# Batches 0 and 1 of a fused sliding-attention and MLP kernel: 1 KB runs for their tokens, fewer clears, weights loaded in eighths between tokens, their mask added by TensorE, and one norm for both dilated heads

## The chip, the cores and the metric

The kernel runs on one core of one Trainium2 chip. The metric is the device time of one execution in microseconds. Engines are named as in the profile: PE (TensorE, matrix multiplications; PEld its weight loads), DVE (VectorE), ACT (ScalarE), POOL (GpSimd), SP (SyncE, which issues nearly all transfers). Each engine works through its own instructions in the order in which they were written; semaphores between engines make an instruction wait for others.

## What is computed

Sliding-window attention, then a two-layer MLP over all 4,608 tokens. Heads 0 to 3 are plain (a query sees the 32 keys up to its own), heads 4 to 7 dilated (32 keys in steps of 4):

```python
# q, k, v: (8 batches, 8 heads, 576 tokens, 64), float32
rel = pos[:, None] - pos[None, :]
mask_plain = (rel >= 0) & (rel < 32)
mask_dil = (rel >= 0) & (rel < 32 * 4) & (rel % 4 == 0)
scores = np.where(masks, 0.125 * q @ k.T, -1e9)
attn = softmax(scores) @ v
x = attn.transpose(0, 2, 1, 3).reshape(4608, 512)
h = x @ w_in                        # 512 -> 2048
out = np.maximum(0.01 * h, h) @ w_out   # 2048 -> 512, float32
```

All matmuls take fp16 operands; inputs are float32 and are cast on the chip.

## The kernel before

**Attention.** Tokens of a head are put in groups of four, 144 groups a batch. A visit is one batch and one pair of heads (hp 0 and 1 plain, 2 and 3 dilated). Its queries and keys are loaded by group (`stg`), cast to fp16 (`nat`), turned by TensorE and copied from PSUM into `qbd` (queries of both heads, block-diagonal, zeros beside them) and `kt` (keys). A unit is a third of a visit: scores on TensorE into the single bank `sps` (L641, L625), exponential on ACT into `ee` (L646), a multiplication of `ee` by a 0/1 mask on DVE or, for batches 0 and 1, DVE or POOL (L660), values on TensorE into `ops` (L680, L670). The value tiles `vp` and `vd` hold ones beside the values, so the sums of the softmax come out too. ACT makes their reciprocal with a logarithm (L688) and an exponential (L691) in `rc`, and DVE multiplies the result into `xt` (L697), once for each head.

**MLP.** A chunk is 384 tokens, three chunks to a pair of batches, 12 in all. An up step (L717) is four matmuls of 384 columns for one of 16 blocks of 128 hidden values, into `hps`; ACT applies the leaky ReLU into `gt` (L724). A down quarter (L757) is four matmuls of 512 columns into `fps`; four of them make 128 tokens, which DVE copies to `osb` (L766) for the store. The two banks `fps` also take warm-up matmuls (L776) and fillers (L831), which keep TensorE running where the planner saw a gap.

**The first two batches** (`EARLY = 2`) are treated apart. Part 0 of a batch is its first 96 groups and part 1 the last 48 (`load_rest`, tile `rest`). Chunk 0 holds part 0 of batch 0, chunk 1 that of batch 1, chunk 2 both parts 1. Dilated heads are loaded in runs of 1 KB (a group of four tokens), plain heads in runs of 256 B (one token). Batches 2 to 7 are loaded in runs of 128 B for queries and keys and turned by DVE (L521, L532).

**Clears** (`clear`, L239). `qbd` and `kt` (all columns), `vst` (the value staging tile, in partitions that no transfer fills), `rest`, and the ones in `vp` and `vd`.

**Weights** (`load_w`). Each matrix comes in four parts of 1 MB, staged in tiles that are free at that time (`wst`, `gt` 1 and 2, `xt` 1) and cast by POOL or DVE.

**What sets the order.** All work is recorded as tasks with a priority, engines that may do it, and an assumed duration; `_Plan.run` simulates the engines and writes the instructions in the order that comes out. For transfers, `took` gives an assumed time by the length of a run. `FIRST` sets the priority of early loads, letter by letter: `b` and `c` are the token groups of batches 0 and 1, `0` and `1` their rests, `i` and `o` the weights of the two layers. `RANKS` gives the priority of the early attention parts, `WHEN` that of later batches. So instructions stand in a fixed order on each engine, and one that waits holds all behind it.

Of the kernel before, what the change touches and what calls it, by code (L numbers as in the profile page):

```python
# [17 lines left out]
FIRST = "b0ico1"  # L18
RANKS = ((-100.0, 1.0), (-50.0, 1.0), (-40.0, 1.0), (-30.0, 1.0))


def _constants():
# [12 lines left out]
    rel1 = 96 + c1 - (32 + p)  # L35
    d1 = (rel1 >= 0) & (rel1 < WIN)
    parts = [ident, first, band, band, d0, d1]
# [95 lines left out]
def kernel(  # L133
# [23 lines left out]
    EARLY = 2  # L157
# [20 lines left out]
    NCON = 128 + 288 + 96 + 48  # L178
# [5 lines left out]
    NST, NNAT, NVS, NV, NT, NE, NR, NO, NG = 5, 3, 4, 3, 6, 4, 3, 3, 3  # L184
    PAD = 32
    stg = [sbuf(f"stg{i}", [128, 1280], FP32) for i in range(NST)]
    nat = [sbuf(f"nat{i}", [128, 1152]) for i in range(NNAT)]
    vst = [sbuf(f"vst{i}", [128, 2048], FP32) for i in range(NVS // 2)]
# [3 lines left out]
    kt = [sbuf(f"kt{i}", [128, PAD + S + 64]) for i in range(NT)]  # L192
# [5 lines left out]
    rest = sbuf("rest", [128, 1792])  # L198
# [16 lines left out]
    def took(n, size):  # L215
        for a, ta, b, tb in ((4, 9.0, 128, 14.0), (128, 14.0, 256, 20.5), (256, 20.5, 1024, 60.0),
                             (1024, 60.0, 2048, 90.0)):
            if size <= b:
                return n * (ta + (tb - ta) * (size - a) / (b - a)) / 16e3
        return n * size / 23.5 / 16e3  # L220

    def load(queue, dst, src, n, size, deps, prio):
        eng = ENG[queue]
        return plan.dma(queue, 0.7 if size == 128 else 0.48, took(n, size), deps,
                        lambda e: eng.dma_start(dst, src), prio,  # L225
                        LATE if prio > -1482 else 0.0)
# [27 lines left out]
    for i in range(NT):  # L254
        p = -1900 + i
        t_zero[i] = ([clear("DVE", qbd[i][64:128, 0:S], 0.33, 0.0, p),
                      clear("DVE", qbd[i][0:64, S:2 * S], 0.33, 0.0, p)],
                     [clear("DVE", kt[i], 0.4, 0.0, p)])
    t_ones = {}
    for i in range(NV):  # L260
        p = -1800 if i == 0 else -700
        t_ones["p", i] = clear("POOL", at(vp[i], 0, 128, D, [128, 12], [1, D]), 0.75, 1.0, p)
        t_ones["d", i] = clear("POOL", at(vd[i], 0, 128, D, [128, 16], [1, D]), 0.95, 1.0, p)
# [11 lines left out]
    kept = {}  # L275

    def v_stage(n, users):

        old = []
        for i in range(n):  # L280
            k, w = ring("VST", NVS, users)
            old = old + w + t_vz[k]
            first = k if i == 0 else first
        return vst[first // 2][:, first % 2 * 1024:first % 2 * 1024 + n * 1024], old

    def heads_of(b, vi):
        if b < EARLY:
            return 2 * vi, 2 * vi + 1
        return 4 * (vi // 2) + vi % 2, 4 * (vi // 2) + vi % 2 + 2

    def load_group(b, g, prio):
# [7 lines left out]
        for o, src in ((0, q), (1, k)):  # L299
# [3 lines left out]
            if early and dil:  # L303
# [15 lines left out]
        vs, v_old = v_stage(1 if early else 2, v_users := [])  # L319
        if dil:  # L320
            lv = [load("SP", at(vs, 0, 96, 0, [256 if early else 512, 4], [1, 256]),
                       dram(v, base, [4 * D, 96], [HS, 4], [1, 256]), 384, 1024, v_old, prio)]
            if not early:
                lv.append(load("SP", at(vs, PAD, 112, 256, [512, 4], [1, 256]),
                               dram(v, base + 256 * D, [4 * D, 80], [HS, 4], [1, 256]),
                               320, 1024, v_old, prio))
        elif early:
            lv = [load("SP", at(vs, PAD, 128, hd * 256, [D, 4], [1, D]),
                       dram(v, base + hd * HS, [D, 96], [96 * D, 4], [1, D]),
                       384, 256, v_old, prio) for hd in range(4)]  # L330
# [5 lines left out]
        for j in range(2):  # L336
            nn, n_old = ring("NAT", NNAT, n_users := [])
            na, c_qk = nat[nn], []
            for o in range(2):
                st, s_users = stage[o]  # L340
                if early and dil:
                    dst = at(na, 0, 96, o * 512, [D, 2], [128, 4], [1, D])
                    src = at(st, 0, 96, j * 512, [256, 2], [D, 4], [1, D])
                    n = 512
                elif early:
                    dst = at(na, 0, 128, o * 384, [128, 3], [1, 128])
                    src = at(st, 0, 128, j * 128, [256, 3], [1, 128])
                    n = 384
                else:
# [8 lines left out]
            full, n = (8, 4 if early else 8) if dil else (6, 4 if early else 6)  # L358
            hd, step = (2 * j, 1) if early else (j, 2)
            c_v = [cast(at(vt, 0, 128, 0, [full * 128, 2], [128, n], [1, D]),  # L360
                        at(vs, 0, 128, hd * n * D, [step * n * D, 2], [D, n], [1, D]), 2 * n * D,
                        (lv if dil or not early else lv[2 * j:2 * j + 2]) + d_old, prio)]
            if not dil:
                c_v.append(cast(at(vt, 0, PAD, 128, [full * 128, 2], [128, n - 1], [1, D]),
                                at(vs, 96, 128, hd * n * D, [step * n * D, 2], [D, n - 1], [1, D]),
# [514 lines left out]
```

## Time and profile before

| | us |
|---|---|
| three runs | 341.18, 345.12, 343.71 |
| their median | 343.71 |
| the profiled execution, time | 340.5 |
| the profiled execution, span | 338.7 |
| mean granted TensorE clock in it | 0.979 |

The span runs from the first to the last instruction of the profile; 1.8 us of the time lie around it. In the profile's rows a group reads: line, engine, operation, output<-inputs with sizes, count, then busy time, mean ns of one, and the idle time of the engine just before, with what ended it. A row of a timeline reads: start in us, duration in us, engine, line, operation, count, and in brackets the idle time before it. The chain of work that ended last gives 63% of the span to PE, 9% to ACT, 7% to DMA, 6% to DVE and 5% to SP's queue.

### The profile page before, as it was taken

What the parts mean: (1) busy time and instruction counts of PE and PEld (TensorE: products, weight loads), DVE (VectorE), ACT (ScalarE), POOL (GpSimd) and SP (SyncE); (2) the same over time, 40 slices, a digit from 0 to 9 for tenths busy, and PEclk for the clock granted to TensorE, in tenths of its full rate; (3) what the DMA queues carried; (4) which work ended last, traced back from release to release, by engine and by line L of the source; (5) the groups of instructions that cost most, each with busy time, mean ns of one, the idle gap of its engine ahead of it and who ended that gap; (6) DMA issues with size and microseconds to landing.
All of it is one profiled execution on the core that took longest, in us unless ns stands there. A gap on an engine that the chain in (4) does not pass through costs nothing.

```text
span 338.7 us, 6427 instructions
## 1 busy us (share of the span) xinstructions
PE 310.6 (92%) x2239; PEld 184.2 (54%) x2239; DVE 189.8 (56%) x449; ACT 233.6 (69%) x522; POOL 140.8 (42%) x194
## 2 busy tenths in 40 slices
PE   7576886899999999999989888999999999999994
PEld 3454553465777666655555545555555555555541
DVE  7788679676688687876656648463444330100011
ACT  2388997485889999986768777777788863334310
POOL 9957538217478566764665655621000000000000
PEclk9859999799999999999999999999999999999999
DMA  8999999999999999999999999931111111111113
GB/s 188 208 316 327 188 313 268 174 217 148 171 188 138 166 158 187 151 154 176 175 153 200 176 144 197 151 79 33 43 50 34 34 31 31 33 40 55 31 31 93
DMA packets 159631, 47.87 MB, mean 141 GB/s; under 512 B 142832, under 2 KB 150896, under 8 KB 159600
## 3 DMA queue, kind: packets, MB, share of 16 engines
q1 hardware_dynamic: 159056, 46.94, 76.7%
q10 hardware_dynamic: 544, 0.54, 0.7%
q8 instruction: 17, 0.28, 0.4%
q14 instruction: 14, 0.11, 0.2%
HBM read 38.02 MB, written 9.44 MB: 140 GB/s over the span
## 4 chain that ended last, share of the span: by engine, by line
PE 63%; ACT 9%; DMA 7%; DVE 6%; SPq 5%; issue 3%; POOL 3%; DVEq 0%; POOLq 0%; ACTq 0%
PE fps L757 29%; PE hps L717 27%; SPq L225 5%; DMA stg<-in_q_dram 4%; PE sps L641 3%; PE ops L680 2%; ACT rc L688 2%; ACT rc L691 2%; DMA vst<-in_v_dram 2%; ACT gt L724 2%; ACT ee L646 2%; DVE xt L697 1%; DMA stg<-in_k_dram 1%; POOL vp L235 1%; ACT qbd L490 1%
## 5 line engine op out<-in xcount | busy, mean ns | idle before, releaser
L717 PE MATMUL hps<-xt,w_in 128*128 128x384 f16 (+1 forms) x832 | 151.3, 314 | 1.3 <-ACT gt L724 1.2
L757 PE MATMUL fps<-w_out,gt 128*128 128x512 f16 x576 | 147.8, 382 | 1.6 <-DVE w_out L235 1.4
L724 ACT ACTIVATE gt<-hps 128x384 f16<-128x384 f32 (+1 forms) x208 | 94.7, 464 | 46.0 <-PE hps L717 44.1
L717 PEld LDWEIGHTS <-w_in 128*128 128x128 f16 x832 | 76.3, 98 | 44.9 <-issue 2.0
L757 PEld LDWEIGHTS <-gt 128*128 128x128 f16 x576 | 54.9, 98 | 49.7 <-issue 3.7
L697 DVE TENSOR_TENSOR xt<-ops,rc 64x192 f16<-64x192 f32 x192 | 61.0, 343 | 31.6 <-ACT rc L691 30.2
L688 ACT ACTIVATE rc<-ops 64x384 f32<-64x384 f32 x96 | 46.5, 487 | 18.0 <-PE ops L680 12.1
L766 DVE COPY osb<-fps 128x512 f32<-128x512 f32 x36 | 24.7, 687 | 60.8 <-PE fps L757 60.5
L646 ACT ACTIVATE ee<-sps 128x384 f16<-128x384 f32 x96 | 46.7, 487 | 9.7 <-PE sps L641 8.7
L660 DVE TENSOR_TENSOR ee<-ee,con 128x384 f16<-128x384 f16 x88 | 39.2, 449 | 24.5 <-ACT ee L646 23.3
L691 ACT ACTIVATE rc<-rc 64x384 f32<-64x384 f32 x96 | 49.5, 517 | 1.5
L526 POOL COPY qbd<-turned 64x576 f16<-64x576 f16 x48 | 34.9, 728 | 26.8 <-DVE turned L521 24.2
L235 POOL CAST nat<-stg 128x576 f16<-128x576 f32 (+2 forms) x54 | 34.5, 665 | 24.9 <-DMA stg<-in_q_dram 19.9
L641 PE MATMUL sps<-qbd,kt 128*128 128x192 f16 x160 | 27.6, 255 | 5.6 <-ACT ee L646 4.3
L235 POOL CAST vp<-vst 128x768 f16<-128x768 f32 (+3 forms) x32 | 23.4, 749 | 15.1 <-DMA vst<-in_v_dram 7.5
L641 PEld LDWEIGHTS <-kt 128*128 128x128 f16 x160 | 15.8, 105 | 16.6 <-issue 6.0
L521 DVE STREAM_TRANSPOSE turned<-nat 128x576 f16<-128x576 f16 x24 | 18.2, 768 | 11.6 <-POOL nat L235 11.4
L532 DVE STREAM_TRANSPOSE kt<-nat 128x576 f16<-128x576 f16 x24 | 18.1, 763 | 7.0 <-POOL nat L235 6.9
L235 POOL CAST vd<-vst 128x1024 f16<-128x1024 f32 (+1 forms) x20 | 18.4, 945 | 6.8 <-DMA vst<-in_v_dram 3.6
L680 PEld LDWEIGHTS <-vp 128*128 128x128 f16 x192 | 13.0, 98 | 13.9 <-issue 3.9
L680 PE MATMUL ops<-ee,vp 128*128 128x96 f16 x192 | 16.0, 206 | 4.8 <-DVE ee L660 2.9
L660 POOL TENSOR_TENSOR ee<-ee,con 128x384 f16<-128x384 f16 x8 | 9.0, 1128 | 12.1 <-ACT ee L646 10.4
(60 smaller groups left out, 151.0 us busy)
## 6 DMA issues: line engine op xcount, KB each, us to landing
stg<-in_q_dram SPq DMA_DIRECT2D x48, 144.0 KB, 5.2
stg<-in_k_dram SPq DMA_DIRECT2D x48, 144.0 KB, 4.6
vst<-in_v_dram SPq DMA_DIRECT2D x6, 576.0 KB, 6.6
vst<-in_v_dram SPq DMA_DIRECT2D x8, 384.0 KB, 5.7
out_dram<-osb SPq DMA_DIRECT2D x16, 192.0 KB, 2.4
vst<-in_v_dram SPq DMA_DIRECT2D x8, 320.0 KB, 5.5
out_dram<-osb SPq DMA_DIRECT2D x24, 96.0 KB, 2.4
gt<-in_moe_w_in_dram SPq DMA_DIRECT2D x2, 1024.0 KB, 11.9
```

What stands on the lines that cost most here:

```text
L235: ENG[e].tensor_copy(out=dst, in_=src)
L526: lambda e, p0=p0, hh=hh: nc.gpsimd.tensor_copy(out=at(qb, p0, p0 + 64, hh * S + o, *od), in_=at(xb, p0, p0 + 64, i, *id_)), prio)
L641: nc.tensor.matmul(st[:, 192 * i:192 * i + 192], ka, qa, start=True, stop=True)
L646: lambda e: nc.scalar.activation(out=et, in_=st[:, 0:384], func=AF.Exp, scale=SCALE), prio + 0.1)
L660: ENG[e].tensor_tensor(out=io, in0=io, in1=mk, op=ALU.mult)
L680: nc.tensor.matmul(ot[:, c:c + 96], va, et[:, c:c + 96], start=True, stop=True)
L688: lambda e: nc.scalar.activation(out=rt, in_=ot[64:128, 0:384], func=AF.Ln),
L691: lambda e: nc.scalar.activation(out=rt, in_=rt, func=AF.Exp, scale=-1.0),
L697: nc.vector.tensor_tensor(out=at(xt[m % 2], h % 2 * 64, h % 2 * 64 + 64, h // 2 * 1152 + x, *o_), in0=at(ot, 0, 64, c, *i_), in1=at(rt, 0, ...
L717: nc.tensor.matmul(ht[:, 0:n], w_in[:, i * DFF + j * 128:i * DFF + j * 128 + 128], at(xt[m % 2], 0, 128, i * 1152 + x0 + x, [1, n]), start ...
L724: lambda e: nc.scalar.activation(out=gt[c % NG][:, j * n_c + x:j * n_c + x + n], in_=ht[:, 0:n], func=AF.Prelu, alpha=0.01),
L757: nc.tensor.matmul(ft, g[:, j * n_c + tt * 128:j * n_c + tt * 128 + 128], w_out[:, j * DM:j * DM + DM], start=(j == 0), stop=(j == NJ - 1))
```

## The change

- Plain heads of batches 0 and 1 are loaded by groups of four tokens too, in runs of 1 KB, for both parts; values of plain heads come at once for the whole batch, in runs of 256 B. The transposes for plain visits take four blocks of 96 like those of the dilated.
- `kt` is cleared only in its first 32 columns. `rest` needs no clear, and `vst` one, which ACT makes. There are seven `qbd`/`kt` pairs instead of six.
- Weights come in 16 parts of 0.5 MB; `FIRST` puts them between the tokens. Part 1 of batch 1 gets rank 20 instead of -30.
- For batches 0 and 1 the mask is not multiplied any more. TensorE first writes 0 or -60000 for each score into `sps` (a matmul of the identity with a table), and the scores are added to it in the bank.
- Dilated units use 96 or 80 keys instead of 128 partitions, for all batches; late dilated values are cast in two instructions instead of one. Heads pair as 4·(hp // 2) + hp % 2 and that plus 2 in all batches, so one DVE instruction norms both heads of a dilated unit; plain units keep two.
- `took` assumes 16 ns instead of 14 for a run of 128 B, 22 instead of 20.5 for 256 B, 100 instead of 90 for 2 KB. The table of constants grows from 560 to 992 columns.

```diff
-FIRST = "b0ico1"
-RANKS = ((-100.0, 1.0), (-50.0, 1.0), (-40.0, 1.0), (-30.0, 1.0))
+FIRST = "bbiii0ciiiciooioooooo1"
+RANKS = ((-100.0, 1.0), (-50.0, 1.0), (-40.0, 1.0), (20.0, 1.0))
...
-                     [clear("DVE", kt[i], 0.4, 0.0, p)])
+                     [clear("DVE", kt[i][:, 0:PAD], 0.1, 0.0, p)])
...
-t_rz = clear("POOL", rest[:, 768:1792], 0.9, 0.0, -1700)
-t_vz = []
-for i in range(NVS):
-    part = vst[i // 2][:, i % 2 * 1024:i % 2 * 1024 + 1024]
-    e = "POOL" if i < 2 else "DVE"
-    t_vz.append([clear(e, part[96:128, :], 0.9, 0.0, -1850),
-                 clear(e, part[0:PAD, :], 0.9, 0.0, -1850)])
+t_vz = add("ACT", 1.4, 0.2, [t_warm],
+           lambda e: nc.scalar.copy(out=at(vst[1], 0, PAD, 0, [512, 3], [1, 512]),
+                                    in_=at(warm, 0, PAD, 0, [0, 3], [1, 512])), -1990)
...
-            elif early:
-                lo = [load(queue, at(st, 0, 128, m * 256, [D, 4], [1, D]),
-                           dram(src, base + m * 128 * D, [D, 128], [HS, 4], [1, D]),
-                           512, 256, s_old, prio) for m in range(3)]
...
+w_home = [(gt[2], 0, None), (gt[2], 1024, None), (wst[0], 0, None), (wst[0], 1024, None),
+          (gt[1], 0, None), (gt[1], 1024, None), (gt[1], 2048, None), (xt[1], 0, None),
+          (xt[1], 1024, None), (wst[0], 0, 2), (wst[0], 1024, 3), (gt[1], 0, 4),
+          (gt[1], 1024, 5), (gt[1], 2048, 6), (xt[1], 0, 7), (xt[1], 1024, 8)]
...
+            if by_pe:
+                if small:
+                    bias = at(con, 0, 128, NMASK + M_D1, [0, 8], [1, 48])
+                elif dil:
+                    bias = at(con, 0, 128, NMASK + M_D0, [0, 4], [1, 96])
+                else:
+                    bias = at(con, 0, 128, NMASK + M_PL + (0 if u == 0 else 96),
+                              [96, 2], [0, 2], [1, 96])
+                nc.tensor.matmul(st[0:kn, 0:384], ident[:, 0:kn], bias, start=True, stop=False)
...
-        t_m = add((("DVE", 0.39), ("POOL", 0.9)) if b < EARLY else "DVE", 0.39, 0.15,
-                  [t_e, t_con], mask, prio + 0.1)
+        t_m = t_e if by_pe else add("DVE", 0.39, 0.15, [t_e, t_con], mask, prio + 0.1)
...
-    gt_free = {1 - NG: w_used[1], 2 - NG: w_used[4]}
+    gt_free = {1 - NG: sum(w_used[11:14], []), 2 - NG: w_used[0] + w_used[1]}
```

DVE at the start of the program, before (numbers behind a name are those of the buffer; stg holds float32 tokens, nat their fp16 form):

```order
L239 MEMSET qbd_85 64x288 x2
L239 MEMSET kt_91 128x336
L239 MEMSET vst_73 32x1024 x4
L235 CAST nat_69<-stg_64 96x2x4x64
L235 CAST nat_69<-stg_66 128x384
```

And with the change:

```order
L241 MEMSET qbd_86 64x288 x2
L241 MEMSET kt_93 128x16
L237 CAST nat_69<-stg_64 96x2x4x64
L237 CAST nat_70<-stg_65 96x2x4x64
L468 COPY qbd_80<-tp 64x4x96
```

The four clears of vst ahead of DVE's first cast are gone, and that of kt is of 16 words instead of 336.

SP's queue from the rest of batch 0 on, before (wst, gt and xt are where weights are staged):

```order
L225 DMA stg_64<-in_q_dram 48x4x256
L225 DMA stg_64<-in_k_dram 48x4x256
L225 DMA wst_110<-in_moe_w_in_dram 128x4x512
L225 DMA gt_102<-in_moe_w_in_dram 128x4x512
L225 DMA gt_103<-in_moe_w_in_dram 128x4x512
L225 DMA xt_100<-in_moe_w_in_dram 128x4x512
L225 DMA stg_65<-in_q_dram 96x4x256
```

And with the change, from the fourth part of the up weights to the last one of them:

```order
L227 DMA wst_112<-in_moe_w_in_dram 128x2x512
L227 DMA gt_104<-in_moe_w_in_dram 128x2x512
L227 DMA vst_72<-in_v_dram 96x4x256
L227 DMA gt_104<-in_moe_w_in_dram 128x2x512
L227 DMA stg_67<-in_q_dram 96x4x256
L227 DMA stg_68<-in_k_dram 96x4x256
L227 DMA vst_73<-in_v_dram 96x12x64 x2
L227 DMA gt_104<-in_moe_w_in_dram 128x2x512
L227 DMA xt_102<-in_moe_w_out_dram 128x2x512
L227 DMA wst_112<-in_moe_w_out_dram 128x2x512
L227 DMA xt_102<-in_moe_w_in_dram 128x2x512
```

The up weights stood together ahead of batch 1's tokens; their last eighths now stand behind those tokens and behind two eighths of the down weights.

ACT where batch 1's part 0 ends, before (rc are reciprocals, gt what leaves the leaky ReLU; gt_102 belongs to chunk 1, whose predecessor's 16 activations all stand further ahead):

```order
L688 ACTIVATE rc_97<-ops_115 64x384
L691 ACTIVATE rc_97<-rc_97 64x384
L490 COPY qbd_84<-tp 64x4x48
L490 COPY kt_90<-tp 128x4x48
L724 ACTIVATE gt_102<-hps_116 128x384
L646 ACTIVATE ee_92<-sps_113 128x384
```

And with the change (gt_103 is chunk 0, gt_104 chunk 1):

```order
L651 ACTIVATE rc_99<-ops_117 64x384
L654 ACTIVATE rc_99<-rc_99 64x384
L685 ACTIVATE gt_103<-hps_118 128x384
L685 ACTIVATE gt_103<-hps_119 128x384
L685 ACTIVATE gt_103<-hps_118 128x384
L685 ACTIVATE gt_103<-hps_119 128x384
L685 ACTIVATE gt_104<-hps_118 128x384
```

Four of chunk 0's activations moved behind the last reciprocal of batch 1's part 0, and the copies for part 1 moved further back.

More of the change, by code (lines that the diff above doesn't have):

```diff
@@ L571, in turn @@
-        k_apart = not (dil and part == 1)
-        tq = add("PE", 0.06 * (4 if dil else 3 if part == 0 else 2), 0.25,
-                 c_qk + [t_con] + q_old, pe_q, prio, 0.2)
-        n_users.append(tq)
-        new = []
-        if dil:
-            w = 96 if part == 0 else 128
-            o, od = lo, [[144, 4], [1, hi - lo]]
-            i, id_ = 0, [[w, 4], [1, hi - lo]]
-        else:
-            o, od, i, id_ = arranged(False, lo, hi)
-            i = 0
-        for hh in range(2):
-            p0 = 64 * hh
-            new.append(move(at(qb, p0, p0 + 64, hh * S + o, *od), at(tpb, p0, p0 + 64, i, *id_),
-                            4 * (hi - lo), [tq] + old + zq, prio))
@@ L587, in turn @@
-        if not k_apart:
-            new.append(move(at(kb, 0, 128, o, *od), at(tpb, 0, 128, 64, *id_), 4 * (hi - lo),
-                            [tq] + old + zk, prio))
-        elif part == 1:
-            new.append(move(kb[:, PAD + 512:PAD + S], tpb[:, 192:256], 64, [tq] + old + zk, prio))
+                    nc.tensor.transpose(bank[:, s * 96:s * 96 + 96],
+                                        na[0:96, c + s * step:c + s * step + 128],
+                                        ident[0:96, 0:96])
```

367 lines of the change are left out of this document (169 added, 198 removed).

## The prediction

> **What bounds the kernel now.** I read the page first, then busy time in stretches, then the timeline of the first 70 us, the groups by shape, the DMA traffic of short windows, and last the chain of the late part.
>
> ```profile
> PE 310.6 (92%) x2239; PEld 184.2 (54%) x2239; DVE 189.8 (56%) x449; ACT 233.6 (69%) x522; POOL 140.8 (42%) x194
> PEclk9859999799999999999999999999999999999999
> 10.00:20.00 10.00, 6.17 (x48) 4.44 (x47) 7.46 (x17) 5.13 (x11) 8.30 (x13) 0.68 1.14 205
> 20.00:30.00 10.00, 7.02 (x73) 5.69 (x73) 8.95 (x25) 9.02 (x23) 6.80 (x9) 0.81 1.04 380
> 50.00:60.00 10.00, 6.11 (x45) 3.18 (x44) 9.67 (x22) 6.82 (x15) 7.84 (x9) 1.00 1.15 288
> 60.00:70.00 10.00, 9.19 (x66) 4.79 (x64) 6.86 (x18) 5.56 (x14) 3.36 (x5) 0.83 1.12 156
> sum 80.00, PE 74.38 PEld 43.21 DVE 50.78 ACT 61.38 POOL 49.05; mean PE 18.60 PEld 10.80 DVE 12.69 ACT 15.35 POOL 12.26
> 212.41 0.65 PE hps L717 x4
> 213.06 0.86 PE fps L757 x4
> ```
>
> The columns of a stretch are PE, PEld, DVE, ACT, POOL, granted clock, DMA share, GB/s; the sum row is that of 140 to 220 us. The last two are from the chain: an up step is 0.65 us, a quarter of a down tile 0.86. TensorE bounds the whole, and it gives time away in two places: about 40 us before 66 us, and 80 - 74.4 = 5.6 us between 140 and 220. Behind 220 it is full.
>
> ```profile
> 7.20 0.62 ACT L233 CAST nat<-stg 96x512 f16<-96x512 f32 x1 [5.19 <-DMA stg<-in_k_dram]
> 7.94 0.91 DVE L239 MEMSET vst<- 32x1024 f32 x1 [0.25 <-DMA stg<-in_q_dram]
> 11.46 0.91 DVE L239 MEMSET vst<- 32x1024 f32 x1 [0.24 <-issue]
> 12.30 0.35 DVE L235 CAST nat<-stg 96x512 f16<-96x512 f32 x1
> 13.09 0.96 ACT L490 COPY qbd<-tp 64x384 f16<-64x384 f16 x2 [3.25 <-PE tp L543]
> 32.50 0.81 PE L717 MATMUL hps<-xt,w_in 128*128 128x384 f16 x4
> 65.05 1.03 PE L757 MATMUL fps<-w_out,gt 128*128 128x512 f16 x4
> 65.91 0.81 PE L717 MATMUL hps<-xt,w_in 128*128 128x384 f16 x4
> 13.00:62.60 49.60, 41.89 (x95) 0.88 1.08 274
> L691 ACT ACTIVATE rc<-rc 64x384 f32<-64x384 f32 x20 | 10.3, 518 | 0.3
> L646 ACT ACTIVATE ee<-sps 128x384 f16<-128x384 f32 x20 | 9.8, 490 | 2.8 <-PE sps L641 2.6
> L688 ACT ACTIVATE rc<-ops 64x384 f32<-64x384 f32 x20 | 9.6, 487 | 2.9 <-PE ops L680 2.5
> L724 ACT ACTIVATE gt<-hps 128x384 f16<-128x384 f32 x16 | 7.5, 490 | 0.5 <-PE hps L717 0.2
> L490 ACT COPY qbd<-tp 64x384 f16<-64x384 f16 x7 | 3.3, 473 | 4.1 <-PE tp L543 3.3 <-DVE qbd L492 0.7
> L490 ACT COPY qbd<-tp 64x192 f16<-64x192 f16 x4 | 1.2, 310 | 0.1
> ```
>
> Queries could have been cast at 7.2 us (keys were), but VectorE stood in its clears until 12.30. From there ScalarE sets the pace (row of 13.00 to 62.60: 41.9 of 49.6 us): 20 units of attention, the last of which lets chunk 1 start, at 65.91. Until 32.50 no useful large matmul ran. So the milestone that I follow is chunk 1's first up step.
>
> **Start of the chain.** VectorE loses the four clears of vst (7.94 to 12.30) and most of each kt clear; two q clears are added.
>
> ```profile
> 1.25 0.30 DVE L239 MEMSET qbd<- 64x288 uint32 x1
> 1.57 0.34 DVE L239 MEMSET kt<- 128x336 uint32 x1
> 2.03 0.30 DVE L239 MEMSET qbd<- 64x288 uint32 x1
> ```
>
> A round of three took 1.16 us; seven rounds without most of kt's 0.34 take about 0.85 each, from 0.86 to 6.8 us (8.9 if a small clear cost as much as a large one). ScalarE's new clear (1,536 columns, at 0.62 us for 512 below 1.9 us) lies in its 5.19 us of waiting. Late next is the key load: the constants ahead of it on ACT's queue grow by 111 KB, 0.5 to 1 us by the rates below, so I put its landing at 8.0, its cast to 8.6 and ScalarE's first copy at 8.7, 4.4 us earlier than 13.09. POOL's clears before its first cast fall too (four of vst, one of rest).
>
> **ScalarE until chunk 1.** By the order it now does 20 units of 0.490 + 0.487 + 0.518 (29.9), 12 of the 16 activations of chunk 0 (5.9), five copies of 0.473 (2.4) and six of about 0.31 (1.9): 40.1 us. It waited 49.6 - 41.9 = 7.7 us. What goes of that is the mask step between exponential and value matmul:
>
> ```profile
> L660 DVE TENSOR_TENSOR ee<-ee,con 128x384 f16<-128x384 f16 x88 | 39.2, 449 | 24.5 <-ACT ee L646 23.3
> L660 POOL TENSOR_TENSOR ee<-ee,con 128x384 f16<-128x384 f16 x8 | 9.0, 1128 | 12.1 <-ACT ee L646 10.4
> L697 DVE TENSOR_TENSOR xt<-ops,rc 64x192 f16<-64x192 f32 x192 | 61.0, 343 | 31.6 <-ACT rc L691 30.2
> ```
>
> 16 of the 88 on VectorE (7.2 us) and all 8 on POOL (9.0 us) go. They stand in each unit's latency; with four exponentials in flight I let 3.2 of the 7.7 us go and keep 4.5 (bounds 0 and 9). So the last reciprocal of batch 1's first part ends at 8.7 + 40.1 + 4.5 = 53.3. Behind it, by ScalarE's order, stand chunk 0's last four activations, and on TensorE two up steps and a down quarter: 53.3 + 0.5 + 2 x 0.65 + 0.86 = 56.0 for chunk 1's first up step, against 65.91. But then only 3 down quarters are done instead of 6 (2.6 us), and four mask matmuls are still to come (4 x 0.16). Net gain 9.9 - 2.6 - 0.6 = **6.7 us** (bounds 2 and 11). By the same count the first up step of all comes at 8.7 + 14.0 (8 units, five copies) + 2 of waiting + 0.7 of norm, near 26, against 32.50.
>
> The second part of batch 1 moves from ahead of chunk 1's steps to among them (its rank goes from -30 to 20): its four units then run beside up and down steps. Plain pairs are turned by four and four transposes instead of three and three, on a TensorE that waits: nothing.
>
> The mask matmul has no row. An up matmul of 384 columns (0.65 / 4 = 0.16 us) is nearest, twice that where the clock is halved: 24 of them, 3.9 to 7.8 us. Twenty lie before chunk 1's start, where TensorE waits for ScalarE; the other four are in the sum. The merged norm for dilated heads is one instruction of twice 192 columns, two of 0.343 at most: VectorE's time falls by up to 0.3 us a unit, beside ScalarE, at nothing. The dilated value cast of late batches becomes two instructions on POOL, 61% busy in 140 to 220: nothing.
>
> **Transfers.** Short windows of nearly one size each:
>
> ```profile
> DMA packets 1715, 0.42 MB, mean 211 GB/s; under 512 B 1715, under 2 KB 1715, under 8 KB 1715
> DMA packets 480, 0.47 MB, mean 233 GB/s; under 512 B 27, under 2 KB 480, under 8 KB 480
> DMA packets 1359, 2.71 MB, mean 387 GB/s; under 512 B 45, under 2 KB 45, under 8 KB 1357
> ```
>
> They are 11 to 13, 33 to 35 and 22 to 29 us: runs of 256 B, 1 KB and 2 KB. Per early batch the change takes 1 KB runs from 1,856 to 3,008 and 256 B runs from 7,168 to 2,304: from 1.90 / 0.233 + 1.83 / 0.211 = 16.9 us to 13.2 + 2.8 = 16.0. That is 0.9 us a batch, since the larger run moves only a tenth faster here. The Trainium skill ("DMA: Bandwidth & Descriptors", Specifications) has line rate from 512 B on and an HBM limit of about 358 GB/s; by it the 1 KB runs would take 8.6 us a batch instead of 13.2, and the sum would be that of rival (d). The trace disagrees: 233.
>
> Weights: up weights in eighths behind tokens. Ahead of the last needed up eighth stand, by SP's order, 5.5 MB of weights and constants at 387 (14.2 us), 5.05 MB of 1 KB runs (21.7) and 1.18 MB of 256 B runs (5.6): with a start near 2.6 and 1.5 of latency it lands near 45.5, 8 us before ScalarE needs it. In the old order all up weights came before batch 1. So the loads hide behind ScalarE, and moving them gains nothing by itself. One wait is new: chunk 1's activations write gt 1, where three down-weight eighths are staged; these land four eighths of 1.35 us later, near 51, and are cast near 53. Late, they would hold ScalarE's queue, with batch 1's second part behind it; 3 us are left.
>
> **Late part.** From 150 to 208 us the chain leaves TensorE:
>
> ```profile
> 155.81 5.19 DMA stg<-in_q_dram
> 182.53 4.58 DMA stg<-in_q_dram
> 200.91 4.58 DMA stg<-in_k_dram
> PE ops L680 <- DVE ee L660: 4.5, 5, 1.4
> ```
>
> The last row is TensorE's waits in 100 to 220 us: the fixed order put late attention where its tokens had not landed. The planner now books 128 B runs at 16 instead of 14 and output rows at 100 instead of 90, so it writes attention later against the matmuls, which leaves fewer such waits. It can also only move them. I take half, **2.8 us** (bounds -2 and 5.6).
>
> **Sum.** 338.7 - 6.7 - 2.8 = 329.2 us of span, with the 1.8 around it (340.5 - 338.7) 331.0. The profiled execution was 0.7 to 4.6 us faster than the three runs, 3.2 than their median; I add 2: **333 us**.
>
> **Rivals.** (a) The transfers pace it: the late chain above runs through loads, so what the start gains is waited for later; only 1.8 us of DMA time are saved: 336.9 of span, 341. For it speaks a DMA share above 1 up to 220 us; against it that TensorE waited only 5.6 of 80 us there. (b) ScalarE waits as before (7.7 us): gain 3.5 + 2.8, about 336. The single score bank now also holds the mask matmul, which speaks for it. (c) Slower: VectorE's queue behind weight casts. By its order the casts of the late eighths stand ahead of batch 1's last norms; if the last up eighth lands after 53 instead of 45.5, norms, output banks and TensorE wait one for one. From 67 on the kernel is more than 1% slower than before; at 70 the time is about 350. That needs transfers to take half as long again as the rows give. (d) 1 KB runs at the 2 KB rate (387): loads far ahead, no late waits: about 330. No row has it, and one row (233) speaks against it; the page on DMA named above would have it so. (e) ScalarE never waits and no late waits: 326.
>
> On the clock: it was 0.68 and 0.81 in 10 to 30 us and 0.83 in 60 to 70, each after thin TensorE work. The Trainium skill ("TensorE: Matmul & The Clock Gate", Part 1) halves the rate after an idle window of about 3.4 us; the trace agrees with the halving. By the order, fillers (L831) ahead of the first up step fall from 57 to 41, so a halved window may fall at chunk 1's start: 1.7 us, inside the range.
>
> **Chances.** Forecast (329 to 337) 0.55; (a) 0.14; (b) 0.12; (c) 0.05; (d) 0.04; (e) 0.10. The range 325 to 341 leaves out (c), half of (e), and part of (a). A measurement of this kernel tells about 1% from no change: faster than 340.3 are the forecast, (b), (d), (e): 0.80; (a) is within 1%: 0.14; slower 0.06.
>
> **What would show it.** In the new profile: VectorE's first cast below 8 us and ScalarE's first copy near 8.7; first up step near 27; chunk 1's first up step near 56; no mask rows before 60 us; ScalarE busy about 90% from 9 to 53; TensorE above 76 of 80 us in 140 to 220. Wrong would be a first up step as late as 32, a w_in cast that VectorE waits for while norms stand behind it, or a 140 to 220 stretch with more idle TensorE than now.

## The result, and the profile after

The changed kernel takes 331.04 us (median of four runs, 328.35 to 332.14) where the old one takes 343.0 (341.18 to 345.12): a ratio of 0.9638, with a 95% interval of 0.9553 to 0.9722. Measured again later, against other runs of the old kernel, it was 0.9647 [0.9607, 0.9687]. The profiled execution took 328.35 us, with a span of 326.5.

The page of the changed kernel: busy time of the engines, the granted clock in 40 slices, and the shares of the chain that ended last.

```profile
PE 309.6 (95%) x2258; PEld 187.3 (57%) x2258; DVE 176.5 (54%) x386; ACT 230.2 (70%) x512; POOL 128.9 (39%) x192
PEclk9699999999999999999999999999999999999998
PE 83%; ACT 9%; DMA 3%; DVE 2%; issue 2%; ACTq 0%; DVEq 0%
```

TensorE's work is about the same (309.6 us against 310.6), in a span that is 12.2 us shorter. Its clock was low in one slice near the start; the second low window that the old profile had near 65 us is not there. The next rows are busy time in stretches of the changed kernel (PE, PEld, DVE, ACT, POOL, granted clock, DMA share, GB/s), and the sum over 140 to 220 us.

```profile
10.20:52.80 42.60, 35.20 (x332) 24.96 (x333) 30.33 (x74) 37.09 (x83) 19.99 (x29) 0.92 1.12 280
60.00:70.00 10.00, 10.00 (x91) 6.31 (x90) 5.76 (x15) 6.82 (x16) 2.44 (x4) 1.00 1.05 155
sum 80.00, PE 79.92 PEld 48.46 DVE 55.95 ACT 69.74 POOL 49.28; mean PE 19.98 PEld 12.12 DVE 13.99 ACT 17.43 POOL 12.32
```

In 140 to 220 us TensorE now idles 0.1 us instead of 5.6. Most of the rest of the 12.2 us is won before 66 us. The timeline of the changed kernel (start, duration, engine, line, operation):

```profile
6.45 0.46 DVE L237 CAST nat<-stg 96x512 f16<-96x512 f32 x1
9.56 0.62 ACT L235 CAST nat<-stg 96x512 f16<-96x512 f32 x1 [6.06 <-DMA stg<-in_k_dram]
10.28 0.47 ACT L466 COPY qbd<-tp 64x384 f16<-64x384 f16 x1
12.27 0.49 ACT L610 ACTIVATE ee<-sps 96x384 f16<-96x384 f32 x1
29.75 1.47 PE L678 MATMUL hps<-xt,w_in 128*128 128x384 f16 x8
52.26 0.52 ACT L654 ACTIVATE rc<-rc 64x384 f32<-64x384 f32 x1
54.64 1.03 PE L718 MATMUL fps<-w_out,gt 128*128 128x512 f16 x4
55.50 0.81 PE L678 MATMUL hps<-xt,w_in 128*128 128x384 f16 x4
```

The last row is chunk 1's first up step, the milestone of the prediction: 55.50 instead of 65.91. The sixth is the last reciprocal of batch 1's first part, which lets it start. So 10.4 us were won there; 3.2 of them are paid back, since three down quarters (3 x 0.86) that used to lie ahead of chunk 1, and four mask matmuls (4 x 0.16) that the old kernel did not have, lie behind its start. That leaves 7.2 us of start and 12.2 - 7.2 = 5.0 behind it. This split is a rough one: by TensorE's idle time alone, 5.2 us went before 66 us and 5.5 between 140 and 220.

### The profile page after: what moved, and what is told of

Read it like the earlier page. It is cut to its first block, busy times and chain, and to the rows that moved or that the text cites. A ratio compares the mean times of both kernels' runs of the same rounds, so it can differ in the third digit from the quotient of the medians.

```text
span 326.5 us, 6336 instructions
## 1 busy us (share of the span) xinstructions
PE 309.6 (95%) x2258; PEld 187.3 (57%) x2258; DVE 176.5 (54%) x386; ACT 230.2 (70%) x512; POOL 128.9 (39%) x192
## 4 chain that ended last, share of the span: by engine, by line
PE 83%; ACT 9%; DMA 3%; DVE 2%; issue 2%; ACTq 0%; DVEq 0%
PE fps L718 38%; PE hps L678 35%; PE sps L604 4%; PE ops L643 3%; DMA stg<-in_k_dram 3%; ACT rc L651 2%; ACT ee L610 2%; ACT rc L654 2%; ACT gt L685 2%; PE sps L588 1%; PE ops L633 1%; PE sps L585 1%; ACT qbd L466 1%; DVE xt L659 0%; DVE ee L624 0%
## 5 line engine op out<-in xcount | busy, mean ns | idle before, releaser
L718 PE MATMUL fps<-w_out,gt 128*128 128x512 f16 x576 | 145.4, 379 | 0.2 <-DVE w_out L237 0.2
L659 DVE TENSOR_TENSOR xt<-ops,rc 64x192 f16<-64x192 f32 (+1 forms) x144 | 56.0, 412 | 38.1 <-ACT rc L654 35.5
L610 ACT ACTIVATE ee<-sps 128x384 f16<-128x384 f32 (+2 forms) x96 | 46.5, 485 | 12.2 <-PE sps L604 9.8
L624 DVE TENSOR_TENSOR ee<-ee,con 128x384 f16<-128x384 f16 (+2 forms) x72 | 33.6, 468 | 31.8 <-ACT ee L610 31.2
L237 POOL CAST nat<-stg 128x576 f16<-128x576 f32 (+1 forms) x55 | 36.2, 679 | 14.8 <-DMA stg<-in_q_dram 7.2
L604 PE MATMUL sps<-qbd,kt 128*128 128x192 f16 (+1 forms) x160 | 27.5, 254 | 0.0
L604 PEld LDWEIGHTS <-kt 128*128 128x128 f16 (+1 forms) x160 | 18.6, 124 | 14.3 <-issue 4.9
L237 POOL CAST vp<-vst 128x768 f16<-128x768 f32 (+1 forms) x32 | 24.4, 786 | 5.9 <-DMA vst<-in_v_dram 5.3
L237 POOL CAST vd<-vst 96x512 f16<-96x512 f32 (+1 forms) x32 | 19.2, 633 | 9.3 <-DMA vst<-in_v_dram 9.2
L643 PE MATMUL ops<-ee,vp 128*128 128x96 f16 x192 | 15.5, 206 | 0.6 <-DVE xt L659 0.5
L585 PE MATMUL sps<-con 128*128 128x384 f16 (+2 forms) x24 | 8.5, 354 | 4.1 <-ACT ee L610 4.1
```

The lines of the kernel that those rows point to most:

```text
L237: ENG[e].tensor_copy(out=dst, in_=src)
L604: nc.tensor.matmul(st[0:kn, 192 * i:192 * i + 192], ka, qa, start=not by_pe, stop=i == 1 or not by_pe)
L610: lambda e: nc.scalar.activation(out=et[0:kn, :], in_=st[0:kn, 0:384], func=AF.Exp, scale=SCALE), prio + 0.1)
L624: ENG[e].tensor_tensor(out=io, in0=io, in1=mk, op=ALU.mult)
L643: nc.tensor.matmul(ot[:, c:c + 96], va, et[0:kn, c:c + 96], start=True, stop=True)
L659: nc.vector.tensor_tensor(out=at(xt[m % 2], h0 % 2 * 64, h0 % 2 * 64 + 64, h0 // 2 * 1152 + x, *o_), in0=at(ot, 0, 64, c, *i_), in1=at(rt, ...
```

## The experiments

Three questions were open: what filled the late part, which of the edits made the start earlier, and whether the two are separate at all. In the table, "idle" is the time in the profiled execution in which TensorE was not busy, and "chunk 1" the start of its first up step, in us. The ratio is to the old kernel.

| kernel | ratio [95%] | chunk 1 | idle 0 to 66 | idle 140 to 220 |
|---|---|---|---|---|
| old | 1 | 65.91 | 17.3 | 5.6 |
| changed | 0.9638 [0.9553, 0.9722] | 55.50 | 12.1 | 0.1 |
| changed, again | 0.9647 [0.9607, 0.9687] | 55.06 | 12.6 | 0.1 |
| old, new transfer costs | 0.9714 [0.9664, 0.9764] | 62.07 | 17.8 | 0.2 |
| changed, old transfer costs | 0.9707 [0.9648, 0.9766] | 58.39 | 12.1 | 2.2 |
| old, allowance of 6 us | 0.9902 [0.9869, 0.9935] | 66.53 | 17.2 | 4.4 |
| old, no clears on VectorE | 0.998 [0.9942, 1.0018] | 64.06 | 17.6 | 5.0 |
| old, clears apart | 1.0015 [0.9987, 1.0042] | 63.23 | 14.1 | 6.2 |
| changed, clears back on VectorE | 0.9732 [0.9686, 0.9778] | 59.94 | 12.9 | 1.7 |
| changed, weights in one line | 0.9708 [0.9661, 0.9755] | 57.90 | 14.3 | 2.3 |
| changed, 256 B runs | 0.9631 [0.9583, 0.9678] | 58.02 | 15.5 | 0.0 |
| changed, mask by VectorE | 0.9571 [0.9531, 0.9611] | 56.94 | 11.3 | 1.0 |
| same, keys first | 0.9619 [0.9576, 0.9663] | 56.82 | 13.6 | 0.1 |
| changed, copies on VectorE | 0.9612 [0.9574, 0.965] | 56.11 | 12.7 | 0.6 |

**The planner's costs.** First the three numbers in `took`, alone and taken back.

```diff
-((4, 9.0, 128, 14.0), (128, 14.0, 256, 20.5), (256, 20.5, 1024, 60.0), (1024, 60.0, 2048, 90.0))
+((4, 9.0, 128, 16.0), (128, 16.0, 256, 22.0), (256, 22.0, 1024, 60.0), (1024, 60.0, 2048, 100.0))
```

> The kernel before with the new transfer times alone. Mine: TensorE's idle time from 140 to 220 us falls from 5.6 to below 2 us, chunk 1's first up step stays at 64 to 68 us, time 1 to 1.7% below the kernel before (337 to 340). Rival: without the rest of the change the late waits stay at 4 us or more and the time is that of before.

> The changed kernel, but the planner's transfer times as before (128 B runs 14, 256 B 20.5, 2 KB 90). Mine: the start keeps its gain (chunk 1's first up step at 55 to 58 us), and the 5.5 us that TensorE won between 140 and 220 us come back as waits: 2.5 to 5.5 us of idle there, time 1 to 1.7% above the changed kernel. Rival (the late waits went because attention starts earlier, or for the one norm and the removed masks, not for the costs): idle there stays below 1 us and the time is the same.

In the old kernel these three numbers alone, which change no work but only its order and the choice of engine, bring 2.9%, where the whole change brings 3.6%. That is more than the 1 to 1.7% expected, and chunk 1 came at 62.07, ahead of the 64 to 68 expected. Taken back in the changed kernel they cost only some 0.6%, less than expected, with 2.2 us of late idle time where 2.5 to 5.5 were expected. The busy time of the old kernel with them, and then of the changed kernel without them, in 140 to 220 us:

```profile
sum 80.00, PE 79.83 PEld 47.62 DVE 60.91 ACT 69.73 POOL 45.63; mean PE 19.96 PEld 11.90 DVE 15.23 ACT 17.43 POOL 11.41
```

```profile
sum 80.00, PE 77.77 PEld 46.01 DVE 53.10 ACT 63.65 POOL 49.97; mean PE 19.44 PEld 11.50 DVE 13.27 ACT 15.91 POOL 12.49
```

The old kernel's late idle time falls from 5.6 to 0.2 us. Its start idles as before (17.8 against 17.3): chunk 1 comes 3.8 us earlier, and three down quarters (2.6 us) that stood ahead of it now stand behind. In the chain of the changed kernel without the new costs, transfers come back:

```profile
165.03 5.04 DMA stg<-in_q_dram
178.61 3.84 DMA stg<-in_q_dram
191.82 4.50 DMA stg<-in_q_dram
210.73 4.44 DMA stg<-in_k_dram
```

With the new costs no load stands in the chain between 138 and 222 us, in either kernel. So the theory on the late part holds in kind, though its sizes were off, and the rival that the costs only move waits falls. But the two halves don't add: the costs alone bring 2.9%, everything else alone 2.9%, both 3.6%.

If late attention is simply written too early, another way to book loads later should do the same. The planner's allowance for the landing of a late load went from 4 to 6 us, in the old kernel:

```diff
-AHEAD, LATE = 5.0, 4.0
+AHEAD, LATE = 5.0, 6.0
```

> The old kernel with the planner's allowance for the landing of a late load raised from 4 to 6 us, and its three transfer costs as they were. Theory (the late waits come from an order that put late attention where its tokens had not landed, so that any way of booking them later does): TensorE busy 78 to 80 of 80 us in 140 to 220 instead of 74.4, the time 1 to 1.7% below the old kernel's. Rival (it is the cost of the rows themselves, which spreads transfers against each other, and not the allowance, that matters): 74 to 76 of 80 us, the time within 0.5%.

One per cent was won, the low end of what the theory expected, but TensorE was busy 75.59 of 80 us, as the rival expected, and the chain still ran through five loads:

```profile
sum 80.00, PE 75.59 PEld 44.29 DVE 53.96 ACT 63.78 POOL 50.56; mean PE 18.90 PEld 11.07 DVE 13.49 ACT 15.95 POOL 12.64
```

```profile
171.12 4.95 DMA stg<-in_q_dram
177.24 6.05 DMA vst<-in_v_dram
189.53 3.02 DMA stg<-in_k_dram
198.49 2.12 DMA stg<-in_q_dram
210.05 4.89 DMA stg<-in_q_dram
```

A fixed allowance is therefore not the same as a cost for each run, which adds up over the loads that queue behind one another. That this adding up is the reason was not tried, nor which of the three numbers does it.

**The mask on TensorE.** The mask of the first two batches was multiplied by VectorE or GpSimd again.

```diff
-by_pe = b < EARLY
+by_pe = False
...
-t_m = t_e if by_pe else add("DVE", 0.39, 0.15, [t_e, t_con], mask, prio + 0.1)
+t_m = add((("DVE", 0.39), ("POOL", 0.9)) if b < EARLY else "DVE", 0.39, 0.15,
+          [t_e, t_con], mask, prio + 0.1)
```

> The changed kernel, but the mask of batches 0 and 1 multiplied by VectorE or GpSimd again, none added by TensorE. Mine: ScalarE waits 2 to 4 us more up to the last reciprocal of batch 1's first part, chunk 1's first up step at 57 to 60 instead of 55.5, time 0.5 to 1.2% above the changed kernel. Rival (the mask matmul on the one score bank costs what the multiplication did): chunk 1's first up step at 55 to 56, the time the same.

The mask matmul brings nothing; without it the kernel is no slower, and perhaps a little faster (0.9571 against 0.9647, with intervals that just touch). Chunk 1 came at 56.94, 1.4 us later and just short of the theory's 57 to 60, but with four down quarters done ahead of it instead of three (0.86 us). The waits of TensorE from 9 to 56 us suggest why (for what, us in total, times, longest). In the changed kernel:

```profile
PE sps L585 <- ACT ee L610: 4.1, 7, 1.6
PE fps L518 <- ACT nat L235: 2.7, 1, 2.7
```

And with the mask by VectorE:

```profile
PE sps L604 <- ACT ee L610: 1.9, 5, 0.8
```

L585 is the mask matmul. It opens the one score bank, which the exponential of the unit before must have emptied. Without it the score matmul (L604) opens the bank, and waits 2.2 us less in total; the value matmuls then wait 0.7 us for the multiplied `ee`. So what the multiplication took out of a unit's round seems to have gone back in as waiting for that bank. This is not proved: the planner wrote another order, and TensorE had waited 3.6 us for the bank in the old kernel too.

**Clears on VectorE.** The old kernel with the clears of the second vst on ScalarE instead of VectorE:

```diff
-e = "POOL" if i < 2 else "DVE"
-t_vz.append([clear(e, part[96:128, :], ...), clear(e, part[0:PAD, :], ...)])
+if i < 2:
+    t_vz.append([clear("POOL", part[96:128, :], ...), clear("POOL", part[0:PAD, :], ...)])
+else:
+    t_vz.append([add("ACT", 1.0, 0.2, [t_warm], ... nc.scalar.copy(...)) for p in (96, 0)])
```

> The kernel before with VectorE's four clears of the value staging tile made by ScalarE in its wait for keys. Mine: VectorE's first cast at 8 to 9 us instead of 12.3, the first exponential about 4 us earlier, but the masks stay between exponential and value matmul, so chunk 1's first up step gains 2 to 4 us (62 to 64) and the time 0.5 to 1.2%. Rival (the transfers of 256 B runs pace the start): the first cast is early and chunk 1's first up step stays at 65 to 66; the time is that of before.

The first cast started at 7.62 instead of 12.30, but the first exponential came at 13.18 instead of 14.97, and the time did not change. The gain was lost in VectorE's casts themselves. Their group in 7 to 13 us (busy, mean ns):

```profile
L235 DVE CAST nat<-stg 96x512 f16<-96x512 f32 x3 | 4.6, 1581 | 0.0
```

In the changed kernel a cast of this shape took 0.46 us. The mean of 1.58 us hides that only one of the three was long: the first, from 7.62 to 11.13, took 3.51 us, and the other two about 0.6 each. GpSimd was clearing without a gap until 10.84, shortly before that first cast ended (its timeline, from 6.76 us):

```profile
6.76 0.94 POOL L239 MEMSET rest<- 128x1024 f16 x1
7.64 0.73 POOL L239 MEMSET vp<- 128x768 f16 x1
8.32 0.94 POOL L239 MEMSET vd<- 128x1024 f16 x1
9.22 0.73 POOL L239 MEMSET vp<- 128x768 f16 x1
9.90 0.94 POOL L239 MEMSET vd<- 128x1024 f16 x1
```

To test this, the last four of these clears went behind GpSimd's first value casts, by a wait of 11 us that exists in the plan alone:

```diff
+t_late = add("X", 11.0, 0.0, [], lambda e: None, 0)
...
-return add(eng, dur, 0.2, [], lambda e: ENG[e].memset(dst, value), prio, 0.0, "set")
+return add(eng, dur, 0.2, [t_late] if prio == -700 else [], lambda e: ENG[e].memset(dst, value), ...)
```

> The old kernel with the four clears of vst on ScalarE, as in the run in which VectorE's first three casts took 4.59 us, and with GpSimd's clears of the second and third vp and vd placed behind its first value casts instead of ahead of them, at 7.6 to 10.8 us. Theory (VectorE's casts stood still while GpSimd cleared): VectorE's casts in 7 to 13 us take 0.4 to 0.7 us each instead of 1.58, the first exponential comes at 10.5 to 12 instead of 13.18, chunk 1's first up step at 62 to 64 instead of 64.06, the time 0.3 to 1% below the old kernel's (0.998 with VectorE's clears alone gone). Rival (the casts were long because their tokens came late): 1.5 us each again, the first exponential near 13, the time 0.998 of the old kernel's.

The same group, and the first exponential:

```profile
L235 DVE CAST nat<-stg 96x512 f16<-96x512 f32 x2 | 1.1, 590 | 0.0
```

```profile
10.30 0.49 ACT L655 ACTIVATE ee<-sps 128x384 f16<-128x384 f32 x1 [0.41 <-PE sps L650]
```

A cast takes 0.59 us (two are on VectorE here, the third on GpSimd), and the first exponential comes 4.7 us earlier than in the old kernel (14.97). So GpSimd's clears had held VectorE. And yet the time is that of the old kernel, within 0.4%: chunk 1 starts 2.7 us earlier, TensorE idles 3.2 us less before 66 us, and from 100 us on it idles more than in the old kernel's profile (38.74 of 40 us busy against 39.58, then 73.79 of 80 against 74.38, and 18.79 of 20 against 19.97; together 2.6 us). Its chain runs through loads as before. The old kernel's profiled execution took 3 us less than its median, so the idle times alone would not carry this; with the equal times they suggest that, with the old costs, a gain in the start is waited for later, as rival (a) had it.

In the changed kernel, where late loads no longer end any wait, four clears of the same size were put back ahead of VectorE's first cast, with no other instruction moved:

```diff
+[clear("DVE", xt[0].bitcast(FP32)[0:32, 0:1024], 0.0, 0.0, -1850) for _ in range(4)]
```

> The changed kernel with four more clears of 32 x 1024 float32 words on VectorE ahead of its first cast (of a buffer that is written later anyway), as the old kernel had them; no instruction moves otherwise. Theory (the first cast sets the start of the chain, but the key load, which lands at 9.56, now takes over what the cast gives up): first cast at 10.1 instead of 6.45, first exponential 1 to 1.5 us later than 12.27, chunk 1's first up step at 56.5 to 57, the time 0.3 to 0.5% above the changed kernel's. Rival (the clears are worth their whole 3.7 us): first exponential at 16, chunk 1 at 59, the time 1.1% above. Second rival (ScalarE's later waits swallow it): chunk 1 within 0.4 us of 55.5.

The first cast came at 11.01, the first exponential at 14.34 instead of 12.27, chunk 1 at 59.94, and the time rose by 0.9% (0.9732 against 0.9647). At chunk 1 and in the time this is nearer to the rival's forecast than to the theory's, though the first exponential lies nearer to the theory's 13.3 to 13.8 than to the rival's 16: 2.1 us there became 4.4 at chunk 1. The clock had a part in that growth. It was 0.55 in 20 to 25 us and 0.66 in 50 to 55, against 1.00 in both in the changed kernel; the down quarter at 53.20 took 1.73 us instead of 1.03, and some 0.9 of the 4.4 us came in that second window. Whether the clears caused the low windows was not separated. The 1.7 us of idle time in 140 to 220 are one wait of 1.6 us for `xt` at 142.02, which in the repeat of the changed kernel stands at 137.13, outside that stretch. The same edit that is worth nothing in the old kernel is worth about 3 us in the changed one.

**Weights mixed with tokens.** All up eighths ahead of batch 1's tokens, as the old kernel had its quarters:

```diff
-FIRST = "bbiii0ciiiciooioooooo1"
+FIRST = "bb0iiiiiiiiccoooooooo1"
```

> The changed kernel with its weights in one line: all eight up eighths after the rest of batch 0 and ahead of batch 1's tokens, then all down eighths behind these tokens, as the old kernel had it in quarters. Theory (the place of the weights is worth nothing by itself, since the loads hide behind ScalarE): chunk 1's first up step at 55 to 57, the time within 0.5% of the changed kernel's. Rival (the mixing is what keeps ScalarE in work): batch 1's keys land about four eighths of 1.35 us later, ScalarE waits some 4 us more between 25 and 45 us, chunk 1's first up step at 59 to 62, the time 1 to 2% above.

The last reciprocal of batch 1's first part ends 4.7 us later (57.46 instead of 52.78). Part of it is made good, because chunk 0's up steps and more of its down quarters are done by then. The time is some 0.6% above the changed kernel's; the intervals overlap a little (0.9661 and 0.9687). That lies between the two forecasts: the place of the weights is worth something, probably about 2 us. By itself the new rank of batch 1's second part (20 instead of -30) does nothing: with -30 the planner writes the same order on every engine.

**Runs of 1 KB.** The plain heads' queries and keys in 256 B runs again, four transfers for one:

```diff
+for m in range(4):
+    eng.dma_start(part(dst, m), part(src, m))
```

> The changed kernel, with the queries and keys of the plain heads of the first two batches (first parts and rests) fetched in 256 B runs again: each of these transfers becomes four, one per token of a group of four, into the same places; the order of all engines stays. Theory (runs of 1 KB move only a tenth faster and the loads hide behind ScalarE): 1,152 runs of 1 KB a batch become 4,608 of 256 B, 1.18 MB at 211 instead of 233 GB/s, 0.5 us of transfer a batch; chunk 1's first up step stays within 0.7 us of 55.5, the time within 0.3% of the changed kernel's. Rival (the long runs are what the start gained by): chunk 1's first up step at 58 or later, the time 0.8 to 2% above the changed kernel's.

No difference in time (0.9631 against 0.9647). Chunk 1 started at 58.02 in the profiled execution, the rival's value, but that execution took 332.3 us, the longest of its six (328.95 to 332.29), and the time decides. Why it came late there stays open: in the two profiled executions of the changed kernel it came at 55.50 and 55.06. Four transfers for one also take four issues on the queue, so the run changes more than the length of a run. The rates agree with those of the prediction. DMA traffic of the changed kernel in 7 to 10 us, nearly all 1 KB runs, and of the one with 256 B runs in 10 to 13:

```profile
DMA packets 732, 0.71 MB, mean 237 GB/s; under 512 B 37, under 2 KB 732, under 8 KB 732
```

```profile
DMA packets 2414, 0.60 MB, mean 201 GB/s; under 512 B 2414, under 2 KB 2414, under 8 KB 2414
```

**An earlier key load.** On top of the mask by VectorE, the unit matrix alone went ahead of the keys on ScalarE's queue, and the masks to SyncE's.

```diff
-t_con = load("ACT", con, const_d, 128, NCON * 2, [], -2000)
+t_con = load("ACT", con[:, 0:128], dram(const_d, 0, [NCON, 128], [1, 128]), 128, 256, [], -2000)
+t_masks = load("SP", con[:, 128:NCON], dram(const_d, 128, [NCON, 128], [1, NMASK]), 128, NMASK * 2, [], -1498.5)
```

> The changed kernel with the mask multiplied by VectorE or GpSimd again, without the table of -60000, and with the constants split: the unit matrix (32 KB) ahead of the keys on ScalarE's queue, the masks (110 KB) on SyncE's queue behind the first values. Theory (the key load, late because of the 254 KB of constants ahead of it, sets the start): keys land at 8.0 to 8.5 instead of 9.56, the first exponential at 11 instead of 12.27, chunk 1's first up step at 54 to 55.5, the time 0.3 to 0.6% below that of the changed kernel with the mask multiplied (0.957 of the old kernel's). Rival (ScalarE's waits further on swallow an earlier start): chunk 1 at 56 to 57 as in that kernel, the time the same as its.

The keys landed at 8.26 instead of 9.14 and the first exponential came at 11.16, as expected; chunk 1 came at 56.82, as without it (56.94), and the time is no better. The rival holds.

**Does ScalarE's work pace the start?** The copies of turned queries and keys on VectorE alone, the weight casts on GpSimd alone:

```diff
-return add((("DVE", 0.1 + n * 0.00065), ("ACT", 0.06 + n * 0.00085)), None, 0.2, deps, fn, prio)
+return add((("DVE", 0.1 + n * 0.00065),), None, 0.2, deps, fn, prio)
...
-WENG = ("POOL", "DVE")
+WENG = ("POOL",)
```

> The changed kernel with the copies of the turned queries and keys on VectorE alone (some eleven of them, 3 to 4 us, were on ScalarE before chunk 1) and the weight casts on GpSimd alone, so that VectorE gets no busier. Theory (ScalarE's own work paces the time until chunk 1): ScalarE's 37 us of work before chunk 1 fall to 33 or 34, chunk 1's first up step comes 2 to 4 us earlier than in the changed kernel, the time falls by 0.5 to 1%. Rival (it is the round of a unit through TensorE, ScalarE and VectorE that paces, and ScalarE's waiting grows by what its work shrinks): chunk 1 within 1 us or later, the time within 0.4% or above.

> The changed kernel once more, unchanged, as the measure for the others: 0.963 of the old kernel's time, with an interval of half a per cent to each side. Both theories expect the late part full again (79.9 of 80 us). If chunk 1's first up step is a property of the fixed order, it comes at 55.5 again within 0.5 us; if it moves from one execution to the next with the landing of the loads, it comes 1 to 3 us elsewhere, as in the kernel with the 256 B runs (58.0 at the same time of run).

Busy time up to the last reciprocal of batch 1's first part, for the changed kernel again and then with the copies on VectorE (ScalarE is the fourth):

```profile
9.90:52.40 42.50, 34.22 (x332) 23.90 (x333) 29.61 (x74) 37.13 (x84) 19.12 (x29) 0.96 1.09 282
```

```profile
9.70:53.40 43.70, 35.18 (x344) 25.06 (x345) 29.47 (x73) 33.84 (x73) 28.43 (x45) 0.96 1.09 283
```

ScalarE lost 3.3 us of work, and its waiting grew from 5.4 to 9.9 us; chunk 1 came 1.05 us later, and the time is the same within the intervals. This is the rival's forecast: ScalarE's own work is not what sets the start. That the round of a unit through TensorE, ScalarE and VectorE sets it is what is left, but no run shows it by itself: the copies went to VectorE, which is in the same round, and the planner wrote another order. So this shows that less work on ScalarE is not enough, not what the best order would do. The changed kernel's second profiled execution had chunk 1 at 55.06 against 55.50, so that in these two it belongs to the order within 0.5 us.

## Why the prediction was right, and where it was not

The time, its sign and the milestone were right: 333 forecast against 331.04, and chunk 1 at 56.0 against 55.50. The split behind the sum was not. In the profiled executions the forecast was 6.7 us of start and 2.8 behind it, and 7.2 and 5.0 came. The 6.7 were near by luck, since errors inside them cancel, as told below.

- **Start of the chain: too early by 1.6 us.** VectorE's first cast came at 6.45, below 8 as forecast, but the keys landed at 9.56 instead of 8.0, and ScalarE's first copy came at 10.28 instead of 8.7. The 4.4 us were 2.8. The prediction also laid the delay to VectorE's clears alone: in the old kernel, taking only these away moved the first exponential by 1.8 us, and moving GpSimd's clears too, by 4.7. The first up step was put near 26 and came at 29.75: TensorE's queue has work ahead of it that waits for the casts of rest, at 24.60 and 27.19, which the count of ScalarE's work left out.
- **ScalarE's 40.1 us: right as a list, wrong as a bound.** The rows of 10 to 53 us add up to 40.5 (20 exponentials, 20 logarithms, 20 reciprocals, 13 activations and the copies). They overlap at their ends, so 37.09 us were busy, with 5.5 of waiting instead of 4.5. These two errors and the late start cancel, which was luck: 52.78 for the last reciprocal against 53.3. The test with less work on ScalarE showed that the bound was not its work.
- **The mask's 3.2 us: wrong.** The step that failed is "what of that goes is the mask step": ScalarE's waiting did fall, from 7.7 to 5.5 us, but it is as low with the mask on VectorE (37.84 of 43 us busy in 10 to 53, against 37.47 with the mask matmul), and the time is no worse. The score bank, which rival (b) named, fits as the reason: TensorE waited 4.1 us for it, against 1.9 without mask matmuls.
- **Late part, 2.8 us: right in mechanism, undersized.** The half that was taken should have been the whole: 5.5 us less idle time in the profiled executions. By the times it is more, 2.9% for the costs alone, a part of it in the start; the old kernel's profiled execution took 340.5 us against medians of 343 to 344, so its row may have shown fewer late waits than most executions have.
- **Runs of 1 KB: right.** A tenth faster and nothing in the time. Rival (d), with 1 KB runs as fast as 2 KB runs and no late waits, forecast about 330, as near to 331.04 as the forecast's 333. The late waits did go, but not by the rate, which was 237 GB/s. The Trainium skill ("DMA: Bandwidth & Descriptors", Specifications) puts line rate at transfers of 512 B and more; these traces do not bear it out.
- **Weights: nothing by itself was probably wrong,** by some 2 us. The last up eighth landed just before its cast at 48.30, not at 45.5, and was in time; GpSimd's last down casts ended at 55.9 without holding ScalarE.
- **Rank 20: wrong.** With -30 the program is the same. The second part of batch 1 kept its time: its rest was cast at 59.72 and 61.63 before, at 60.68 and 63.88 after. It was chunk 1 that moved ahead of it.
- **Clock.** The halved window feared at chunk 1's start did not come: the granted clock was 1.00 from 20 us on in both profiled executions of the changed kernel. With the four clears back, such a window did come, 0.66 in 50 to 55 us.
- **Rival (a): too simple.** It fits the old kernel with its old costs, where an earlier start brought nothing, and not the changed one. In the sum, start and late part were added as if apart, and they are not: 2.9% and 2.9% make 3.6%.

What stays open: which of the three costs matters, why the late idle time is 2.2 us in one order with the old costs and 5.6 in another, and how the start's gain divides. Taken back one at a time, the clears are worth 0.9%, the weights' places and the costs 0.6% each, the runs nothing and the mask less than nothing, of 3.5% in all by the repeat. No run takes back the single norm for dilated heads, the 96 or 80 keys, the smaller clears of `kt` or the seventh `qbd`/`kt` pair.

## What to carry to other kernels

Where a planner writes a fixed order, its assumed transfer times are part of the kernel: three numbers alone were worth as much as all other edits without them, so set them by the waits on loads in the chain, before anything is rebuilt. Test a gain at the start in a kernel whose late part no longer waits for loads; the same four clears cost nothing in one and 0.9% in the other. And before counting an engine's work as the bound, take some of it away: an engine that is busy 87% of a stretch need not be what sets its length.

## What the runs showed of the hardware

A VectorE cast of float32 to fp16 stood still while GpSimd filled memory: in the old kernel without VectorE's clears it started at 7.62 us, within a train of clears without a gap, and ended at 11.13, 0.29 us after the last of them; casts of this shape took 0.35 to 0.62 us without such a train. VectorE's own clears don't collide with GpSimd's: 32 x 1024 words took 0.91 us each beside them in the old kernel, and 0.91 with GpSimd idle (in the changed kernel with the four clears back, at 6.63). The Trainium skill ("SBUF — State Buffer", Who interferes with whom) has this rule: casts can enter a mode that takes the port pair shared with GpSimd, and the one that comes second blocks for the whole instruction, while other VectorE instructions with at most one input don't contend. The traces agree with both halves, and here the wait lasted through the rest of the train, four more clears, and not through one instruction.

1 KB runs to 96 partitions moved at 233 to 237 GB/s here, near the 201 to 211 of 256 B runs and far from the 387 of 2 KB runs. 256 B runs moved at 211 to 128 partitions and at 201 to 96. For 1 KB and 2 KB runs, partitions and run length changed together, so the cause was not separated.
